# Moving the queries to the compressive memory from the projections into turns of the attention, in an attention pair on one core

## The chip, the core and the metric

One Trainium2 chip; the program runs on one of its cores. A core has TensorE (PE; its weight loads are shown as PEld), VectorE (DVE), ScalarE (ACT), GpSimd (POOL) and SyncE (SP, which here only issues DMAs); each takes its own instructions in order. The metric is device time in microseconds of a whole execution, median over runs.

## What is computed

Two attention layers stand side by side, each with 2048 tokens, 576 channels and 32 heads of 18. Their outputs are joined along the channels. A is attention of all queries over one shared head of keys and values. B works in four segments of 512 tokens: causal attention within the segment, and for each head a memory (M, z) gathered from the segments before, mixed by a gate.

```python
# A
scores = jnp.einsum("bhqd,bkd->bhqk", q, k) * (Dh ** -0.5)
o_A = jnp.einsum("bhqk,bkd->bhqd", softmax(scores), v)      # then @ wo
# B, phi(t) = t + 1 if t > 0 else exp(t), g = sigmoid(beta)
for s in range(4):
    a_dot = softmax(qs @ ks.T * scale + mask) @ vs
    num = jnp.einsum("bhld,bhde->bhle", phi(qs), M)
    den = jnp.einsum("bhld,bhd->bhl", phi(qs), z)[..., None] + 1e-6
    o = g * num / den + (1.0 - g) * a_dot                   # then @ wo
    M = M + jnp.einsum("bhld,bhle->bhde", phi(ks), vs)
    z = z + jnp.einsum("bhld->bhd", phi(ks))
```

## The kernel before

**Projections (to about 314 us).** Heads are held in five tiles of rows, four with 7 heads (126 rows) and one with 4 (72 rows); RT has the rows, t counts the tiles. Inputs and weights are split in two parts, so a projection of 512 tokens is 14 matmuls (`proj`, L239). A's four chunks come first, then B's four segments: keys and the last query tile, values (`values`, L467), the other query tiles, the bound on the scores (L530), and the update of the memory (L555 to L571). Queries, keys and values go to DRAM. For segments 1 to 3 the memory is asked here: `phi` makes phi(q) of a tile, `from_memory` multiplies it by the block-diagonal Mst (L407), scales by the gate (L411) and stores the numerator to `numB` (L412); when all five tiles are there, five products with zst (L521) give the denominators, stored to `denB` (L526). Each of these float32 products shows as two records.

**Attention (from about 314 us).** A has 32 blocks (chunk, group of four heads) of 16 key tiles, B 32 blocks of 3. The order of blocks is written out: A0, four blocks of B, A1, four of B, A2, two of B, A3, four of B, A4, two of B and so on. A block's work is cut in items (key tile, pair of heads) and these in turns of three, so an A block has 11 turns and a B block two. The first turns are 0 to 10 (A0), 11 to 18 (B), 19 to 29 (A1), 30 to 37 (B), 38 to 48 (A2), 49 to 52 (B), 53 to 63 (A3). In turn k the loop issues, in this order: the scores of turn k on PE (L845 for A, L854 for B) and their exponentials on ACT (L863), the middle one through a copy by DVE (L860); one step of the fill; one step of DVE's own exponentials; the products of turn k - 2 with the values (L893, four column tiles of 32); and what is due from a list of later steps. One item of every A block, (0, 1), has its exponential on DVE, as a polynomial of ten instructions (L818 to L828). POOL masks B's diagonals (L868).

**The fill** is the output projection of finished chunks. `out_proj` gives 60 steps of four matmuls (L742) into the single PSUM bank F; `run_fill(1)` takes one per turn. What is left at the end is made up in the tail, before the last chunk's output.

**The later steps.** When a chunk's heads 0 to 27 or 28 to 31 are done, `finish` sets down, counted in turns: d0 until the softmax sums are loaded, d1 until their inverses, d2 from a tile of heads (`load_heads`, into the tile "o" of two buffers) until its weights are loaded (tiles "rb" of ten buffers), d3 until POOL weighs it (L729). Two turns after the fifth tile, `out_proj` is put into the fill.

**Order.** PE, ACT and DVE take the attention's instructions in the order of the code (`manual_schedule`). SP's and POOL's order is made by a planner that takes the earliest instruction in the code's order whose inputs and memory it holds to be free by its own costs. A tile gets its memory from a pool, and the pools of the attention lie over those of the projections. "stA" and "P" are in one pool (`pp`), "stB", "vseg", "o", "rb", "woA" and "woB" in another (`pa`).

**Loads at the start.** Queries and keys of eight heads at a time make a stack; stB and stA have two buffers each, and the next stack is asked for when a new one is begun:

```python
    prefetch("B", 1)
    load_vseg(0)
    prefetch("B", 2)
    prefetch("A", 2)
```

A's first stack (st0) is loaded during the projections. B's output weights are loaded in turn 5, A's in turn 24.

## Time and profile before

| | us |
|---|---|
| median of three runs | 1448.38 (1448.08 to 1453.36) |
| the profiled execution | 1452.01 |
| its span, from the first to the last instruction | 1450.0 |
| PE busy in the span | 1424.0 (98%) |
| ACT busy | 1194.9 (82%) |
| DVE busy | 1023.9 (71%) |
| POOL busy | 245.7 (17%) |

Lines of the profile's views read as follows. A row of the timeline has the start and the duration in us, the engine (SPq is SP's queue of DMA issues), the line of the kernel, the operation, out<-in by the tiles' names, partitions and elements, a count where neighbours are merged, and in brackets how long the engine had been idle and what ended it. A row of the groups has the same names, a count, the busy time in us, the mean in ns of one, and the idle time before them. A row of the windows has the stretch, its length, and for PE, PEld, DVE, ACT and POOL the busy time and the number of instructions; then TensorE's granted clock, the DMA engines' busy share, and GB/s. A row of windows for one source line has PE and PEld alone. Matmuls are pipelined: the duration of one is longer than the step to the next, so costs are read from start to start.

### The profile page before, as it was taken

To read this page: it belongs to the slowest core of one execution; us is meant where nothing else is said; L and a number is where in the kernel's file an instruction comes from. 1 tells how busy PE (TensorE), PEld (TensorE's weight loads), DVE (VectorE), ACT (ScalarE), POOL (GpSimd) and SP (SyncE) were. 2 spreads that over 40 slices of the span, in tenths; PEclk is the share of its full clock that TensorE was granted. 3 is DMA by queue.
4 is the path that set the end of the run, shared out by engine and by line. 5 is a ranking of instruction groups with operands and counts; after the bars stand their busy time and mean duration, and the time that the engine had idled before them with its cause. 6 is when DMAs were issued, how large, how long until landed. Compare 5 with 4: busy or idle time off the path is not lost.

```text
span 1450.0 us, 40761 instructions
## 1 busy us (share of the span) xinstructions
PE 1424.0 (98%) x17540; PEld 840.9 (58%) x17540; DVE 1023.9 (71%) x1211; ACT 1194.9 (82%) x1429; POOL 245.7 (17%) x324
## 2 busy tenths in 40 slices
PE   9989999999999999999999999999999999999998
PEld 6768878855454555555555555555555555555565
DVE  6663473556776678887777788777778877887761
ACT  4542334259999999999999999999999999999960
POOL 2421000002123312311110160131013300100001
PEclk9999999999999999999999999999999999999999
DMA  9864444457465335332312452123104121110022
GB/s 278 270 215 137 130 162 159 162 165 202 147 175 159 92 97 175 116 108 87 108 57 68 128 154 80 62 100 93 57 26 143 60 74 46 57 42 17 17 87 74
DMA packets 86079, 166.33 MB, mean 115 GB/s; under 512 B 11872, under 2 KB 19673, under 8 KB 85718
## 3 DMA queue, kind: packets, MB, share of 16 engines
q1 hardware_dynamic: 79014, 152.87, 33.8%
q0 software_dynamic: 1664, 4.78, 1.3%
q10 hardware_dynamic: 5216, 6.03, 1.3%
q8 instruction: 138, 2.26, 0.7%
q14 instruction: 47, 0.39, 0.1%
HBM read 96.15 MB, written 67.49 MB: 113 GB/s over the span
## 4 chain that ended last, share of the span: by engine, by line
PE 64%; ACT 8%; DMA 3%; issue 2%; DVE 0%; POOL 0%; SPq 0%; DVEq 0%; POOLq 0%; ACTq 0%
PE O L893 30%; PE E L845 19%; PE F L742 11%; ACT P L863 8%; PE E L854 3%; PE E L742 1%; DMA sm<-oB 1%; PE O L742 1%; DMA rB<-sm 0%; DMA rA<-sm 0%; DMA stA<-qA 0%; DMA stB<-kB 0%; DMA stB<-qB 0%; DMA out<-osb 0%; DMA rb<-rB 0%
## 5 line engine op out<-in xcount | busy, mean ns | idle before, releaser
L863 ACT ACTIVATE P<-E 128x1024 f32<-128x1024 f32 (+1 forms) x800 | 788.4, 1078 | 15.0 <-PE E L845 11.8
L860 DVE COPY W<-E 128x1024 f32<-128x1024 f32 (+1 forms) x384 | 461.0, 1201 | 188.6 <-PE E L845 121.4
L893 PE MATMUL O<-P,VA 128*32 128x256 f32 x7936 | 509.7, 380 | 0.0
L863 ACT ACTIVATE P<-W 128x1024 f32<-128x1024 f32 (+1 forms) x384 | 434.6, 1132 | 1.5 <-DVE W L860 1.5
L893 PEld LDWEIGHTS O<-P,VA 128*32 128x32 f32 x7936 | 262.6, 110 | 146.6 <-issue 9.5
L845 PE MATMUL E<-stA,kstA 56*128 56x512 f32 x1920 | 330.8, 440 | 2.0 <-ACT P L863 1.3
L845 PEld LDWEIGHTS E<-stA,kstA 56*128 56x128 f32 x1920 | 154.6, 184 | 180.8 <-ACT P L863 121.0
L868 POOL TENSOR_SCALAR_AFFINE_SELECT P<-P 128x256 f32<-128x256 f32 (+1 forms) x192 | 94.2, 493 | 447.5 <-ACT P L863 414.7
L729 POOL TENSOR_TENSOR o<-o,rb 126x512 f32<-126x512 f32 (+1 forms) x40 | 60.5, 1518 | 436.8 <-PE F L742 143.5
L742 PE MATMUL F<-woB,o 126*32 126x192 f32 (+1 forms) x1920 | 127.6, 338 | 0.0
L825 DVE SCALAR_TENSOR_TENSOR q<-q,PD 128x1024 f32<-128x1024 f32 x96 | 118.5, 1234 | 0.0
L893 PE MATMUL O<-P,vseg 128*32 128x256 f32 (+2 forms) x1536 | 83.4, 348 | 1.9 <-POOL P L868 1.8
L742 PEld LDWEIGHTS F<-woB,o 126*32 126x32 f32 (+1 forms) x1920 | 38.2, 108 | 70.8 <-issue 61.4
L742 PE MATMUL F<-woA,o 126*32 126x192 f32 (+1 forms) x1240 | 77.7, 338 | 1.3 <-DVE osb L767 1.3
L111 ACT CAST qp<-pj 126x512 fp32r<-126x512 f32 (+1 forms) x54 | 31.3, 583 | 54.6 <-DVE kmB L423 33.2
L239 PE MATMUL pj<-xh,wBh 128*126 128x512 f32 x180 | 75.0, 416 | 0.0
L902 DVE COPY oe<-O 128x512 f32<-128x512 f32 x64 | 44.2, 691 | 41.7 <-PE O L893 39.3
L239 PE MATMUL pj<-xh,wBl 128*126 128x512 f32 x180 | 72.9, 405 | 0.0
L112 DVE TENSOR_TENSOR qp<-pj,qp 126x512 fp32r<-126x512 f32 (+1 forms) x54 | 36.7, 684 | 49.7 <-ACT qp L111 49.6
L854 PE MATMUL E<-stB 56*128 56x256 f32 (+3 forms) x512 | 62.5, 350 | 2.5 <-ACT P L863 2.0
L893 PEld LDWEIGHTS O<-P,vseg 128*32 128x32 f32 x1536 | 48.6, 110 | 27.9 <-issue 3.3
L239 PE MATMUL pj<-xl,wBh 128*126 128x512 f32 x144 | 60.0, 417 | 0.0
(177 smaller groups left out, 1372.7 us busy)
## 6 DMA issues: line engine op xcount, KB each, us to landing
stB<-kB SPq DMA_DIRECT2D x96, 144.0 KB
stB<-qB SPq DMA_DIRECT2D x32, 288.0 KB
stA<-qA SPq DMA_DIRECT2D x30, 288.0 KB
oA<-oe SPq DMA_DIRECT2D x32, 256.0 KB
oB<-oe SPq DMA_DIRECT2D x32, 256.0 KB
qA<-qp SPq DMA_DIRECT2D x16, 504.0 KB
kB<-qp SPq DMA_DIRECT2D x16, 504.0 KB
qB<-qp SPq DMA_DIRECT2D x16, 504.0 KB
```

What stands on the lines that cost most here:

```text
L112: nc.vector.tensor_tensor(qp[:R, 1, :n], src, qp[:R, 0, :n].bitcast(F32), op=ALU.subtract)
L239: nc.tensor.matmul(dst, w[:, c0 : c0 + M], x, start=i == 0, stop=i == len(ops) - 1)
L729: steps = [lambda: v.tensor_tensor(o, o, rb, op=ALU.mult)]
L742: nc.tensor.matmul(dst[32 * j : 32 * j + 32], parts[ab, c][: RT[t], t, r0 : r0 + 32], wo[ab][: RT[t], t, c0 : c0 + n], start=start, stop=stop,
L825: steps.append(lambda a=a: v.scalar_tensor_tensor(q, q, a, p, op0=ALU.add, op1=ALU.mult))
L845: nc.tensor.matmul(e[:, j], kstA[rows, 128 * kt : 128 * kt + 128], st[rows, h, :], start=True, stop=True)
L854: nc.tensor.matmul(e[:, j, c0 : c0 + 512 - 128 * k], st[rows, 4 + h, ks], st[rows, h, 128 * k :], start=True, stop=True)
L860: nc.vector.tensor_copy(src[:, :, :n], e[:, :, :n])
L863: nc.scalar.activation(p[:, :, :n], src[:, :, :n], AF.Exp, scale=SCALE)
L868: nc.gpsimd.affine_select(diag, diag, pattern=[[0, 2], [0, m], [1, 128]], base=0, channel_multiplier=-1, compare_op=ALU.is_ge, fill=0.0)
L893: nc.tensor.matmul(o[32 * j : 32 * j + 32, q0 : q0 + n], v, p[:, j % 2, p0 : p0 + n], start=m == hf == 0, stop=last and hf == 1,)
L902: nc.vector.tensor_copy(osb, o)
```

## The change

The projections no longer ask the memory. They store phi(q) of segments 1 to 3 (`qfB`, 15 stores in place of those to `numB`) and, after each update, M and z (`mzB`, two stores per segment). The matmuls of L407 and L521, their evictions and the stores to `numB` and `denB` leave the projections. Mst and zst are cleared once by POOL.

In the attention a generator `from_memory` asks the memory in 36 half tiles. For each segment these are the denominators of four tiles (t = -1) and the five tiles of numerators, the last with its own denominators; each in two halves of 256 tokens, four matmuls of 32 columns per half, into the bank F. DVE scales or adds 1e-6 and stores follow from SP. A half tile is taken in each turn from 5 on (`ASK`) whose items are all A's, in place of the fill, until all are done: turns 5 to 10, 19 to 29, 38 to 48, 53 to 60. phi(q) of a segment is loaded into a buffer of "o" (segment 1 at the start, 2 in turn 7, 3 in turn 27), M and z into the memory of woA; A's output weights are loaded in turn 92.

Blocks A0, A1 and A2 (`PLAIN`) do all their exponentials on ACT. For B's segment 0 d2 and d3 are 4 and 8 in place of 3 and 6. The heads of a new chunk are loaded only when the buffer of "o" is no longer needed for phi(q) (`place`).

```diff
+MZ = 126 + 32
+ASK, PLAIN = 5, 3
...
+    qfB = {s: dram(f"qfB{s}", [128, 5, C], F32) for s in range(1, NSEG)}
+    mzB = dram("mzB", [128, NSEG - 1, 5, MZ], F32)
...
+        nc.gpsimd.memset(Mst, 0.0)
+        nc.gpsimd.memset(zst, 0.0)
...
-            def from_memory(t):
-                R = RT[t]
-                pn = ps.tile([128, C], F32, name="mm", bufs=1)
-                nc.tensor.matmul(
-                    pn[:R], Mst[:R, t].rearrange("p h d -> p (h d)")[:, :R], fs[t][:R], start=True, stop=True
-                )
-                nm = p2.tile([128, C], F32, name="nm", bufs=2)
-                nc.vector.tensor_scalar(nm[:R], pn[:R], gt[:R, t : t + 1], None, op0=ALU.mult)
-                nc.sync.dma_start(numB[s][126 * t : 126 * t + R], nm[:R])
+            def for_memory(t):
+                nc.sync.dma_start(qfB[s][: RT[t], t], fs[t][: RT[t]])
...
-            if s:
-                pd = ps.tile([128, C], F32, name="nd", bufs=2)
-                for t in range(5):
-                    R = RT[t]
-                    nc.tensor.matmul(
-                        pd[32 * (t % 4) : 32 * (t % 4) + 32], zst[:R, t], fs[t][:R], start=t < 4, stop=t > 0
-                    )
-                dn = p2.tile([128, C], F32, name="ph_e", bufs=2)
-                nc.vector.tensor_scalar(dn, pd, 1e-6, None, op0=ALU.add)
-                nc.sync.dma_start(denB[s], dn)
...
+                nc.sync.dma_start(mzB[:, s, :, :126], Mst.rearrange("p t h d -> p t (h d)"))
+                nc.sync.dma_start(mzB[:, s, :, 126:], zst)
...
+    def load_qf(s):
+        qfs[s] = pa.tile([128, 5, C], F32, name="o", bufs=2)
+        nc.sync.dma_start(qfs[s][:126, :4], qfB[s][:126, :4])
+        nc.sync.dma_start(qfs[s][: RT[4], 4], qfB[s][: RT[4], 4])
+
+    def from_memory():
+
+        mz = pa.tile([128, 5, D], F32, name="woA").rearrange("p t d -> p (t d)")[:, : (NSEG - 1) * 5 * MZ]
+        nc.sync.dma_start(mz, mzB.rearrange("p s t m -> p (s t m)"))
+        mz = mz.rearrange("p (s t m) -> p s t m", t=5, m=MZ)
+        yield None
+        for s in range(1, NSEG):
+            qf = qfs[s]
+            for t in (-1, 0, 1, 2, 3, 4):
+                pf = psO.tile([128, C], F32, name="F")
+                for hf in range(2):
+                    cs = slice(256 * hf, 256 * hf + 256)
+                    if t < 0:
+                        cols = [(32 * i, i, 126, 32) for i in range(4)]
+                    else:
+                        cols = [(32 * j, t, 32 * j, min(32, RT[t] - 32 * j)) for j in range(4) if 32 * j < RT[t]]
+                        if t == 4:
+                            cols.append((96, 4, 126, 32))
+                    for r, i, m, n in cols:
+                        R = RT[i]
+                        nc.tensor.matmul(pf[r : r + n, cs], mz[:R, s - 1, i, m : m + n], qf[:R, i, cs], start=True, stop=True)
+                    if not hf:
+                        yield False
+                if t >= 0:
+                    R = RT[t]
+                    nc.vector.tensor_scalar(qf[:R, t], pf[:R], gt[:R, t : t + 1], None, op0=ALU.mult)
+                    nc.sync.dma_start(numB[s][126 * t : 126 * t + R], qf[:R, t])
...
+                yield True
...
+    def plain(c, hg):
+
+        return 8 * c + hg < PLAIN
...
-        dve = ab == "A" and (kt, pr) in BY_DVE
+        dve = ab == "A" and (kt, pr) in BY_DVE and not plain(c, hg)
...
     prefetch("B", 2)
+    load_qf(1)
+    memory = from_memory()
+    next(memory)
     prefetch("A", 2)
...
-        d0, d1, d2, d3 = (0, 2, 0, 3) if last else (2, 5, 3, 6)
+        d0, d1, d2, d3 = (0, 2, 0, 3) if last else (2, 5, 4, 8) if (ab, c) == ("B", 0) else (2, 5, 3, 6)
...
-            return (ab, c) in parts or len(parts) - filled[0] // FILL < 2
+            return (ab, c) in parts or len(parts) - filled[0] // FILL < 2 and asked[0] >= min(NSEG - 1, len(parts) + 2)
...
+        at(ASK + 2, 0, lambda: True, lambda k: load_qf(2))
...
-            run_fill(1)
+            if memory is None:
+                run_fill(1)
+            elif k >= ASK and k < len(turns) and all(its[n][0] == "A" for n, pr in turns[k]):
+                done = next(memory, None)
+                if done is None:
+                    memory = None
+                    run_fill(1)
+                elif asked[0] == 1 and 3 not in third:
+                    third.add(3)
+                    at(k + 3, 0, lambda: True, lambda k: load_qf(3))
...
-                    if it in (("A", 0, 0, 8), ("A", 0, 1, 8)):
+                    if it in (("A", 0, 0, 8), ("A", 0, 5, 8)):
```

More of the change, by code (lines that the diff above doesn't have):

```diff
@@ L442, in attention_pair_kernel @@
             if s:
-                from_memory(4)
+                for_memory(4)
             if s == 0:
@@ L514, in attention_pair_kernel @@
                     fs[t] = phi(pj[:126], 126, "qf", 5)
[L515 to L526 removed]
+                    for_memory(t)
             pu = ps.tile([128, C], F32, name="nd", bufs=2)
@@ L770, in out_proj @@
                 yield True
+    asked, qfs, third = [0], {}, set()
+    def load_qf(s):
[28 more added lines that the diff above has]
+                    nc.sync.dma_start(numB[s][126 * t : 126 * t + R], qf[:R, t])
+                if t < 0 or t == 4:
+                    r, n = (0, 128) if t < 0 else (96, 32)
+                    dn = pa.tile([128, C], F32, name="rb", bufs=10)
+                    nc.vector.tensor_scalar(dn[r : r + n], pf[r : r + n], 1e-6, None, op0=ALU.add)
+                    if t < 0:
+                        nc.sync.dma_start(denB[s], dn)
+                    else:
+                        nc.sync.dma_start(denB[s][7:11], dn[103:107])
+                if t == 4:
+                    asked[0] = s
+                yield True
     fill, filled, ending = [], [0], []
@@ L845, in scores @@
                 nc.tensor.matmul(e[:, j], kstA[rows, 128 * kt : 128 * kt + 128], st[rows, h, :], start=True, stop=True)
-            if (kt, pr) in BY_DVE:
+            if dve:
                 exponentials(p, e)
@@ L884, in products @@
         for j in range(4):
-            kt = turn_of[j // 2][m] if ab == "A" else m
+            kt = turn_of[j // 2][m] if ab == "A" and not plain(c, hg) else m
             p = state[b + (kt,), j // 2]
```

1 line of the change is left out of this document (removed).

## The prediction

> **What bounds the kernel now.** I read the busy time by stage first, because one average over the span hides two different kernels.
>
> ```profile
> 200.00:250.00 50.00, 50.00 (x290) 42.28 (x290) 27.48 (x68) 20.37 (x43) 0.35 (x1) 1.00 0.45 147
> 340.00:360.00 20.00, 19.21 (x268) 10.78 (x266) 11.79 (x12) 20.00 (x26) 8.87 (x18) 1.00 0.70 200
> ```
>
> In the projections (to about 314 us) PE is full and nothing else is near it. In attention's first turns ACT is full (20.00 of 20) and PE nearly so. Next the groups that the change takes out of the projections:
>
> ```profile
> L407 PE MATMUL mm<-qf,Mst 126*126 126x512 f32 x24 | 12.6, 606 | 0.0
> L521 PE MATMUL nd<-qf,zst 126*32 126x512 f32 x24 | 8.4, 605 | 0.0
> ```
>
> (each product is two records; the 72-row forms add 3.1 us to either group), and the timeline of PE around them in segment 1:
>
> ```profile
> 196.19 0.39 PE L239 MATMUL pj<-xh,wBh 128*126 128x512 f32 x1
> 196.42 1.02 PE L407 MATMUL mm<-qf,Mst 126*126 126x512 f32 x2
> 197.38 1.05 PE L521 MATMUL nd<-qf,zst 126*32 126x512 f32 x4
> 198.36 0.50 PE L239 MATMUL pj<-xl,wBh 128*126 128x512 f32 x1
> 198.69 0.39 PE L239 MATMUL pj<-xh,wBl 128*126 128x512 f32 x1
> ```
>
> Last, the start of attention: what SP issues, and what ACT and PE do meanwhile.
>
> ```profile
> 317.84 0.36 SPq L131 DMA_DIRECT2D stA<-qA  x1
> 318.56 0.31 SPq L131 DMA_DIRECT2D stB<-qB  x1
> 332.60 7.85 SPq L141 DMA_DIRECT2D stB<-shB  x4
> 346.39 0.28 SPq L132 DMA_DIRECT2D stA<-qA  x1
> ```
> ```profile
> 314.60:327.90 13.30, 7.09 (x30) 3.49 (x30) 0.74 0.54 131
> ```
> ```profile
> 327.94 1.08 PE L845 MATMUL E<-st,kstA 56*128 56x512 f32 x6
> 328.95 1.57 PE L893 MATMUL O<-P,VA 128*32 128x256 f32 x24
> 330.45 1.33 PE L845 MATMUL E<-st,kstA 56*128 56x512 f32 x6
> ```
> ```profile
> 329.28 1.96 ACT L863 ACTIVATE P<-E 128x1024 f32<-128x1024 f32 x2
> 332.03 1.07 ACT L863 ACTIVATE P<-E 128x1024 f32<-128x1024 f32 x1
> ```
>
> Apart from one early piece of A's stack, SP issues in the order of the code: B's first stack, the values, B's second stack, the rest of A's. It is at the rest of A's at 346.39. Six score matmuls make a turn; the window row counts 30 of them (L845) before 327.9, five turns, so 327.94 is turn 5 and 330.45 turn 6. ACT does a turn of three exponentials in 332.03 - 329.28 = 2.75 us, 0.918 each.
>
> **The change part by part.** *1. The projections lose the asking.* From 196.19 to 198.69 stand two steps of L239 that take 0.23 each when nothing is between (196.42 - 196.19), so one numerator tile and four denominator records cost 2.50 - 0.46 = 2.04. One numerator tile by itself:
>
> ```profile
> 183.09 0.40 PE L239 MATMUL pj<-xh,wBh 128*126 128x512 f32 x1
> 183.32 1.08 PE L407 MATMUL mm<-qf,Mst 126*126 126x512 f32 x2
> 183.83 0.80 PE L239 MATMUL pj<-xl,wBh 128*126 128x512 f32 x1
> 184.47 0.40 PE L239 MATMUL pj<-xh,wBl 128*126 128x512 f32 x1
> ```
>
> 1.38 - 0.46 = 0.92. So a denominator record costs (2.04 - 0.92) / 4 = 0.28. Three segments have 15 tiles and 30 records: 13.8 + 8.4 = 22.2. Since PE is full, nearly all of it should come off; I take **-21.5**. Bounds: -27 by the groups' busy time, -17 if PE meets waits that this work covers today. In exchange SP gets 15 stores of phi(q) of the size of the 15 numerator stores that go, and six stores of M and z for three of denominators; with the transfers at 0.45 of their time there I cost them at nothing, like the two memsets on an idle POOL. If SP lagged there, the q and k stores behind it would be late, and only the last segment's could then show, by a few us.
>
> *2. Attention has to wait for its new loads.* The code puts phi(q) of segment 1 (1.03 and 0.15 MB by their shapes) and M and z (1.21 MB) behind B's second stack. SP gets there where it issues the rest of A's stack today, 346.39. PE needs them right after the scores of turn 5, at 328.95: its order is fixed, so the products of turn 3 and the scores of turn 6 stand behind the waiting matmul, ACT has only turn 5 left (to about 333), and DVE and POOL wait for ACT. When do 2.4 MB land? The rates of the transfers in that stretch:
>
> ```profile
> 333.00:336.00 3.00, 2.83 (x35) 1.38 (x30) 2.10 (x3) 3.00 (x5) 0.00 (x0) 1.00 0.94 319
> 348.00:351.00 3.00, 2.99 (x48) 1.50 (x36) 1.87 (x2) 3.00 (x5) 2.07 (x5) 1.00 0.68 197
> 354.00:357.00 3.00, 2.97 (x49) 1.85 (x52) 2.00 (x3) 3.00 (x5) 1.97 (x4) 1.00 0.98 269
> ```
>
> At 240 GB/s, between the three, they take 10 us: landed at 357. At 319 it is 354, at 197, with the last of B's keys ahead of them, 361. Their rows are long (8 and 9 KB), which speaks for the faster half; the keys ahead speak for the slower. Restarted, PE is slow, as after its pause at 313:
>
> ```profile
> 320.20 2.79 PE L893 MATMUL O<-P,VA 128*32 128x256 f32 x24
> 324.18 1.50 PE L893 MATMUL O<-P,VA 128*32 128x256 f32 x24
> ```
> ```profile
> 319.00:320.00 1.00, 0.95 (x4) 0.51 (x4) 1.00 (x1) 1.00 (x2) 0.00 (x0) 0.50 0.51 162
> ```
>
> The granted clock is 0.50, and the same 24 records take 2.79 in place of 1.50. So turn 6 is scored at 357 + 0.9 (a half tile has 8 records, 2.79 / 3) + 2.8 = 360.7 where it was 330.45: **+30**. Bounds: +22 (landed by 351 and no slow clock: 351 + 0.5 + 1.5 - 330.45) and +34 (landed at 361); nothing if the loads come first (a rival).
>
> The Trainium skill would land the loads sooner (DMA: Bandwidth & Descriptors, Bandwidth, Measured): 1 MB in 6.15 us, 341 GB/s, on a quiet chip. By that estimate 2.4 MB take 7 us and the whole sum falls by 3; no window of this stretch reaches that rate.
>
> *3. 36 turns get a half tile.* It runs in turns 5 to 10 (A's block 0), 19 to 29, 38 to 48 and 53 to 60, and at 61 the fill takes over. Once attention is full, a turn reads:
>
> ```profile
> 572.85 0.95 PE L845 MATMUL E<-stA,kstA 56*128 56x512 f32 x6
> 573.74 0.53 PE L742 MATMUL F<-woB,o 126*32 126x192 f32 x8
> 574.08 1.48 PE L893 MATMUL O<-P,VA 128*32 128x256 f32 x24
> 575.50 0.97 PE L845 MATMUL E<-stA,kstA 56*128 56x512 f32 x6
> ```
>
> 0.89 + 0.34 + 1.42 = 2.65, PE back to back. A half tile has the shape of a third of the products: 1.42 / 3 = 0.47, so a turn with it takes PE 2.78. Without fill ACT sets the turn: 31 exponentials over 11 turns, 31 x 0.918 / 11 = 2.59. So up to 0.19 x 35 = 6.6 us more; at the least nothing, if PE's slack in these turns takes it. I take **+5**. This covers the third edit too: with 32 exponentials on ACT in blocks 0 to 2 a block takes 29.4, a turn 2.67, still below 2.78. Were PE the faster one, it would cost 3 x 0.918 = 2.75. The ten polynomial instructions that DVE loses per block, for one copy, ran beside ACT (DVE is busy 11.79 of 20 above), and the evictions that it gets (15 tiles and 6 denominators) fit there. The stores of these tiles join SP's queue.
>
> *4. The fill starts later.* By the turn numbers (heads of B's segment 0 weighed at 58 instead of 55, memory done at 61) it starts 3 steps later, and those are made up in the tail:
>
> ```profile
> 1408.43 1.84 PE L742 MATMUL F<-woA,o 126*32 126x192 f32 x40
> 1410.06 1.84 PE L742 MATMUL O<-woA,o 126*32 126x192 f32 x40
> ```
>
> 40 records are five steps and take 1.63, PE without a gap: 3 x 0.33 = **+1**. A's output weights load some 90 turns before they are used; no cost, and a stall of a load's length if not.
>
> *5. B's segment 0 gets slack.* Today POOL's weighing waits for the inverses and B's masks stand behind it:
>
> ```profile
> 440.80 1.29 POOL L729 TENSOR_TENSOR o<-o,rb 126x512 f32<-126x512 f32 x1 [25.77 <-DMA rb<-rB]
> 450.24 1.51 ACT L863 ACTIVATE P<-E 128x768 f32<-128x768 f32 x2 [3.04 <-PE E L854]
> ```
>
> ACT loses 3.04 us. Later weighing may clear this; but its heads now wait for a buffer that the memory's second segment holds until turn 44, which may move it into the masks again. Between -3 and +4; I take 0.
>
> **Sum:** -21.5 + 30 + 5 + 1 + 0 = +14.5 on the profiled span of 1450.0 (its execution took 1452.01; the runs' median is 1448.38). On the median: **1463 us**, 1.0% slower. The likeliest case's own range is 1453 to 1474.
>
> **The rivals.** *Loads in time* (0.13): SP sends phi(q) and M before B's stacks, or PE meets them ready. For it: B's stacks are needed only at turn 11, and one piece of A's stack does overtake. Against: that piece goes to another pool's memory; B's stacks and the new loads share one. Then no stall but the slow start's 2 us: -21.5 + 5 + 1 + 2 = -13.5, **1435**. This ends on the other side, and it decides as soon as the loads are issued before about 322 (7 to 10 us to land before 329 to 332).
>
> *Half the stall* (0.09): the loads land around 348, because SP gets through B's second stack sooner (at 332.60 it stands 7.85 us over four small loads). 22 + 5 + 1 - 21.5 = +6.5, and with the 3 us of part 5 off about **1452**: no change. For it is only that wait.
>
> *SP loses its lead* (0.08): besides the stall. SP runs ahead of the turns today:
>
> ```profile
> 368.55 2.96 SPq L675 DMA_DIRECT2D woA<-a_wo  x5
> 371.61 0.32 SPq L131 DMA_DIRECT2D stB<-qB  x1
> ```
>
> The code asks for this stack in turn 30, and 371.61 is 16 turns of 2.75 behind turn 5. If the stores of the tiles, which wait for DVE turn by turn, stand before such loads, a stack has four turns, some 10 us, for what took (346.39 - 318.56) / 2 = 14 at the start: 4 us at each of three places, 12 in all, **1475**. It decides once a lead falls under 14 us. Against it: SP takes what is ready, and the stall gives it 25 us of lead.
>
> **How the numbers follow.** The forecast has 0.70, the rivals 0.13, 0.09 and 0.08. A change under 0.5% (7.2 us) can't be told from none here: faster is below 1441, slower above 1456. Faster gets nearly all of the first rival, 0.12; no change most of the second, 0.01 of the first and the low edge of the forecast, 0.12; slower the rest, 0.76. The range has to take in the first rival to leave out no more than 2 in 10: 1434 to 1474.
>
> **What would show it.** The two L407 and L521 groups gone and attention starting near 293 in place of 314.6 (step 1). A gap of 24 to 28 us on ACT after its 18th exponential, ended by PE's F, whose matmul waited for the load of M and z; the granted clock at 0.50 behind it (step 2). Turns of 2.78 in blocks 1 and 2 (step 3). The first fill near turn 61 (step 4), and a gap on ACT near turn 52 or none (step 5). No gap at turn 5 makes the forecast wrong, and so does one under 15 us.

## The result, and the profile after

| | before | after |
|---|---|---|
| median of the runs (us) | 1451.33 (six runs, 1448.08 to 1453.36) | 1489.35 (six runs, 1487.80 to 1493.05) |
| ratio, with its 95% interval | | 1.0267 (1.0249 to 1.0286) |
| the profiled execution | 1452.01 | 1488.46 |
| its span | 1450.0 | 1486.7 |
| PE / ACT / DVE busy | 1424.0 / 1194.9 / 1023.9 | 1418.8 / 1198.2 / 1001.0 |

The change made the kernel 2.7% slower: 36.7 us of span, where the prediction had 14.5. PE is busy for 5 us less, so the time went into waits.

**Where the time went.** Everything of the attention runs in one fixed order on DVE, and every block ends with one copy of its output from PSUM (L902 before, L945 after). So the n-th such copy can be set against the n-th of the other kernel, and the difference of the two is the lag up to that block. Here are, from the timelines, the first exponential and the ends of A's block 0, of the fourth block of B behind it, of the first and the second block of B in the next group, of A's block 2, of the second block of B behind that, and of the last block. First the kernel before:

```profile
315.26 3.95 ACT L863 ACTIVATE P<-E 128x1024 f32<-128x1024 f32 x4 [1.34 <-PE E L845]
348.80 0.69 DVE L902 COPY oe<-O 128x512 f32<-128x512 f32 x1 [0.83 <-DMA stB<-kB]
367.46 0.69 DVE L902 COPY oe<-O 128x512 f32<-128x512 f32 x1 [0.43 <-PE O L893]
400.75 0.69 DVE L902 COPY oe<-O 128x512 f32<-128x512 f32 x1 [0.34 <-PE O L893]
405.22 0.69 DVE L902 COPY oe<-O 128x512 f32<-128x512 f32 x1 [0.59 <-PE O L893]
443.56 0.69 DVE L902 COPY oe<-O 128x512 f32<-128x512 f32 x1 [0.78 <-PE O L893]
456.04 0.69 DVE L902 COPY oe<-O 128x512 f32<-128x512 f32 x1
1404.01 0.69 DVE L902 COPY oe<-O 128x512 f32<-128x512 f32 x1 [3.31 <-PE O L893]
```

and the same places after:

```profile
300.50 1.94 ACT L906 ACTIVATE P<-E 128x1024 f32<-128x1024 f32 x2 [7.03 <-PE E L888]
366.63 0.69 DVE L945 COPY oe<-O 128x512 f32<-128x512 f32 x1 [0.73 <-PE O L936]
385.95 0.68 DVE L945 COPY oe<-O 128x512 f32<-128x512 f32 x1
419.62 0.69 DVE L945 COPY oe<-O 128x512 f32<-128x512 f32 x1 [0.34 <-PE O L936]
435.46 0.69 DVE L945 COPY oe<-O 128x512 f32<-128x512 f32 x1 [0.87 <-PE O L936]
474.18 0.69 DVE L945 COPY oe<-O 128x512 f32<-128x512 f32 x1 [0.78 <-DMA o<-oB]
491.42 0.68 DVE L945 COPY oe<-O 128x512 f32<-128x512 f32 x1
1439.76 0.69 DVE L945 COPY oe<-O 128x512 f32<-128x512 f32 x1 [0.94 <-PE O L936]
```

| up to | lag (us) | step | what lies in it |
|---|---|---|---|
| first exponential | -14.8 | -14.8 | projections, and the passage to the attention |
| end of A's block 0 | +17.8 | +32.6 | the wait at turn 5, and the slow start behind it |
| fourth block of B | +18.5 | +0.7 | |
| first block of B's next group | +18.9 | +0.4 | A's block 1 with half tiles |
| second block of that group | +30.2 | +11.3 | a wait in front of turn 34 |
| A's block 2 | +30.6 | +0.4 | half tiles again |
| second block behind it | +35.4 | +4.8 | a wait in front of turn 52 |
| last block | +35.7 | +0.3 | the other 51 blocks |
| end of the span | +36.7 | +1.0 | the tail |

A step is the difference of two rounded lags. All of the loss but 1.3 us is in by 491 us. Behind that the kernels run alike for 950 us, and the ledger leaves four places to read.

**The passage.** After, from the timeline, SP's last store of the segment (shB), ACT's last copy of the projections and PE's first scores (the first exponential stands above); last, the same store and copy of the kernel before:

```profile
291.89 1.48 SPq L526 DMA_DIRECT2D shB<-shp  x1
293.08 0.40 ACT L470 COPY vch<-pj 128x288 f32<-128x288 f32 x1 [1.46 <-PE pj L468]
298.25 0.76 PE L888 MATMUL E<-st,kstA 56*128 56x512 f32 x1 [5.21 <-DMA shB<-shp]
299.71 1.61 PE L888 MATMUL E<-st,kstA 56*128 56x512 f32 x5 [0.69 <-SPq L573]
```
```profile
307.98 0.38 SPq L535 DMA_DIRECT2D shB<-shp  x1
313.52 0.40 ACT L469 COPY vch<-pj 128x288 f32<-128x288 f32 x1 [1.47 <-PE pj L467]
```

The copy comes 20.4 us earlier, nearly the 21.5 of the prediction. But from it to the first exponential it is 1.74 us before and 7.42 after (300.50 - 293.08). PE is through with the projections and waits for the last store of the segment (shB) to land, then for SP, which stands at the branch (L573) in eight waits from 295.3 to 299.8, probably for its last stores to land. The store left SP 5.5 us ahead of ACT's last copy before the change (313.52 - 307.98), and PE worked on the values meanwhile; after, it leaves 1.2 us ahead.

**The wait at turn 5.** After: SP's issues from the start of the attention, PE's first half tile, and ACT's gap.

```profile
303.02 0.36 SPq L137 DMA_DIRECT2D stB<-qB  x1
315.67 8.48 SPq L147 DMA_DIRECT2D stB<-shB  x4
330.11 0.31 SPq L769 DMA_DIRECT2D o<-qfB  x1
330.88 0.36 SPq L775 DMA_DIRECT2D woA<-mzB  x1
344.90 1.08 PE L792 MATMUL F<-o,woA 126*32 126x256 f32 x8 [30.45 <-DMA woA<-mzB]
346.85 1.06 ACT L906 ACTIVATE P<-W 128x1024 f32<-128x1024 f32 x1 [30.19 <-PE O L936]
```

SP spends 27 us on B's two stacks and the values, and only then issues the loads for which PE has been waiting since 314.4. They need 14 us. A window of the stretch (columns as before: the granted clock, the DMA engines' share and GB/s stand last) says that the transfers are not what is scarce: while SP works through the second stack the DMA engines are half idle (0.55 here, 0.38 in the next 5 us), and the clock is at 0.50.

```profile
320.00:325.00 5.00, 0.00 (x0) 0.00 (x0) 0.00 (x0) 0.00 (x0) 0.00 (x0) 0.50 0.55 129
```

**The wait in front of turn 34.** Counted by its exponentials, the gap stands before the first of turn 34, where B's fourth stack comes into use (the expectations below, written before it was counted, say turn 32). After: SP, PE and ACT.

```profile
408.15 0.31 SPq L798 DMA_DIRECT2D numB<-o  x1
408.64 0.31 SPq L769 DMA_DIRECT2D o<-qfB  x1
409.43 0.38 SPq L137 DMA_DIRECT2D stB<-qB  x1
425.97 0.76 PE L897 MATMUL E<-stB 56*128 56x512 f32 x1 [6.42 <-DMA stB<-ones_d]
429.42 1.72 ACT L906 ACTIVATE P<-E 128x1024 f32<-128x1024 f32 x2 [8.63 <-PE E L897]
```

B's fourth stack, issued at 371.61 before, is issued at 409.43, behind the load of phi(q) of segment 3 and stores of half tiles, each of which waits on SP for DVE in its turn (19.5 us of such waits between 380 and 412). PE waits 6.42 us for one piece of it and 1.8 for the next.

**The wait in front of turn 52** ("near turn 50" in the expectations). After, from POOL's timeline and ACT's:

```profile
476.73 1.27 POOL L722 TENSOR_TENSOR o<-o,rb 126x512 f32<-126x512 f32 x1 [31.76 <-DMA rb<-rB]
479.56 3.52 POOL L911 TENSOR_SCALAR_AFFINE_SELECT P<-P 128x256 f32<-128x256 f32 x8
483.71 1.56 ACT L906 ACTIVATE P<-E 128x768 f32<-128x768 f32 x2 [5.89 <-PE E L897]
```

The same picture as before the change (3.04 us there): POOL waits for the inverses with a weighing, and eight masks pile up behind it. The inverses come later now: the weighing starts 35.9 us later than before (440.80 there), where the lag at that place is 30.6. ACT's gap is 2.9 us longer; what makes up the other 1.9 us of this step was not followed.

**The turns.** After, A's block 1, from PE's timeline:

```profile
391.53 0.97 PE L888 MATMUL E<-st,kstA 56*128 56x512 f32 x6
392.43 0.64 PE L792 MATMUL F<-o,woA 72*32 72x256 f32 x8
392.88 1.49 PE L936 MATMUL O<-P,VA 128*32 128x256 f32 x24
394.30 0.98 PE L888 MATMUL E<-st,kstA 56*128 56x512 f32 x6
```

A turn with a half tile takes 394.30 - 391.53 = 2.77 us, the 2.78 of the prediction. From 389 to 400 both PE and ACT are busy for 11.00 of 11 us.

### The profile page after: what moved, and what is told of

It is laid out like the page before. It is cut to its first block, busy times and chain, and to the rows that moved or that the text cites. A ratio compares the mean times of both kernels' runs of the same rounds, so it can differ in the third digit from the quotient of the medians.

```text
span 1486.7 us, 41304 instructions
## 1 busy us (share of the span) xinstructions
PE 1418.8 (95%) x17768; PEld 843.8 (57%) x17768; DVE 1001.0 (67%) x1190; ACT 1198.2 (81%) x1432; POOL 246.4 (17%) x326
## 4 chain that ended last, share of the span: by engine, by line
PE 65%; ACT 6%; DMA 5%; issue 2%; DVE 1%; SPq 1%; POOL 0%; POOLq 0%; DVEq 0%; ACTq 0%
PE O L936 30%; PE E L888 19%; PE F L735 10%; ACT P L906 6%; PE E L897 3%; DMA stB<-qB 2%; PE F L792 1%; PE E L735 1%; DMA woA<-mzB 1%; DMA stB<-kB 1%; DMA rb<-rB 1%; PE O L735 1%; DMA rA<-sm 0%; DVE W L903 0%; SPq L659 0%
## 5 line engine op out<-in xcount | busy, mean ns | idle before, releaser
L906 ACT ACTIVATE P<-E 128x1024 f32<-128x1024 f32 (+1 forms) x800 | 784.1, 1066 | 35.7 <-PE E L888 19.5
L906 ACT ACTIVATE P<-W 128x1024 f32<-128x1024 f32 (+1 forms) x387 | 432.7, 1118 | 32.5 <-PE O L936 30.2
L735 PE MATMUL F<-woB,o 126*32 126x192 f32 x1880 | 125.1, 338 | 0.0
L868 DVE SCALAR_TENSOR_TENSOR q<-q,PD 128x1024 f32<-128x1024 f32 x87 | 110.6, 1271 | 0.0
L735 PEld LDWEIGHTS F<-woB,o 126*32 126x32 f32 x1880 | 37.2, 108 | 69.0 <-issue 60.4
L945 DVE COPY oe<-O 128x512 f32<-128x512 f32 x64 | 44.2, 691 | 39.9 <-PE O L936 38.3
L117 ACT CAST qp<-pj 126x512 fp32r<-126x512 f32 (+1 forms) x54 | 31.0, 583 | 42.9 <-DVE kmB L424 30.2
L897 PEld LDWEIGHTS E<-stB 56*128 56x128 f32 x512 | 40.0, 191 | 39.0 <-ACT P L906 18.8
```

The costliest lines, as they stand in the source:

```text
L735: nc.tensor.matmul(dst[32 * j : 32 * j + 32], parts[ab, c][: RT[t], t, r0 : r0 + 32], wo[ab][: RT[t], t, c0 : c0 + n], start=start, stop=stop,
L868: steps.append(lambda a=a: v.scalar_tensor_tensor(q, q, a, p, op0=ALU.add, op1=ALU.mult))
L897: nc.tensor.matmul(e[:, j, c0 : c0 + 512 - 128 * k], st[rows, 4 + h, ks], st[rows, h, 128 * k :], start=True, stop=True)
L906: nc.scalar.activation(p[:, :, :n], src[:, :, :n], AF.Exp, scale=SCALE)
L945: nc.vector.tensor_copy(osb, o)
```

## The experiments

Kernels with the same projections end them up to 3 us apart from one execution to the next (ACT's last copy at 293.1 in the changed kernel, at 296.3 in the latest of the others), so a single end time can't tell 4 us. The column "attention" below takes that out: the start of the last block's copy less the start of the first exponential, both from the trace of the one profiled execution. "Passage" is the first exponential less ACT's last copy of the projections.

| kernel | end (us) | attention | passage | gaps on ACT in the attention, over 2 us |
|---|---|---|---|---|
| before | 1451.33 | 1088.7 | 1.7 | 3.0 at 52 |
| the change | 1489.35 | 1139.3 | 7.4 | 30.2 at turn 5, 8.6 at 34, 5.9 at 52 |
| loads_first | 1462.32 | 1111.9 | 6.8 | 3.0 in turn 21, 8.0 at 34, 5.3 at 52 |
| early_stacks | 1497.52 | 1146.9 | 7.2 | 28.8 at 5, 9.0 in A's block 2, 6.8 at 52, two of 3.2 and 2.4 later |
| pool_stores | 1485.45 | 1134.9 | 6.9 | 30.2 at 5, 6.9 at 52, 4.0 in A's block 3 |
| no_phi3 | 1486.47 | 1137.0 | 6.2 | as the change; 4.4 at 52 |
| act_loads | 1460.34 | 1107.8 | 8.5 | 8.5 at 34, 5.8 at 52 |
| act_pool | 1463.80 | 1111.5 | 9.2 | 3.3 at 5, 7.3 at 52, 4.0 in A's block 3 |
| late_weigh | 1493.54 | 1138.9 | 8.4 | as the change |
| plain0 | 1489.58 | 1138.7 | 6.9 | as the change; 4.4 at 52 |
| act_third | 1448.80 | 1097.0 | 8.0 | 2.1 in turn 21, 5.7 at 52 |
| third_pool | 1443.91 (9 runs) | 1093.0 | 9.3 | 2.4 in turn 21 |
| seg3_proj | 1445.36 (10 runs) | 1092.2 | 1.7 | none |
| pool_loads | 1446.95 (12 runs) | 1094.4 | 6.8 | 2.9 in turn 21 |

Without a count the end is that of one execution; before and the change have six runs each. The kernel before itself took 1452.65 us beside the kernels from loads_first to no_phi3, 1447.53 beside those from act_loads to plain0 (one execution each), and as the median of 17 runs 1450.07 beside those from act_third to seg3_proj and 1449.28 beside pool_loads.

**The wait at turn 5: loads_first and act_loads.** The first puts the loads ahead of B's stacks on SP, the second leaves SP's order and gives them to ACT's queue.

```diff
+    load_qf(1)
+    memory = from_memory()
+    next(memory)
     prefetch("B", 1)
     load_vseg(0)
     prefetch("B", 2)
-    load_qf(1)
-    memory = from_memory()
-    next(memory)
     prefetch("A", 2)
```

> The changed kernel with phi(q) of segment 1 and M and z loaded ahead of B's two stacks and the values. Theory (the gap of 30 us at turn 5 is only the place of these loads in SP's order): the gap goes, the first half tile finds its data, about 1457 to 1460 us. Rival (the stretch is short of transfer time whatever the order: some 2.4 MB more have to land before turn 15): the gap moves to B's first stack at turn 11, 10 us or more of it come back there, 1468 us or more.

```diff
     def load_qf(s):
+        queue = nc.scalar if s == 1 else nc.sync
         qfs[s] = pa.tile([128, 5, C], F32, name="o", bufs=2)
-        nc.sync.dma_start(qfs[s][:126, :4], qfB[s][:126, :4])
-        nc.sync.dma_start(qfs[s][: RT[4], 4], qfB[s][: RT[4], 4])
+        queue.dma_start(qfs[s][:126, :4], qfB[s][:126, :4])
+        queue.dma_start(qfs[s][: RT[4], 4], qfB[s][: RT[4], 4])
...
-        nc.sync.dma_start(mz, mzB.rearrange("p s t m -> p (s t m)"))
+        nc.scalar.dma_start(mz, mzB.rearrange("p s t m -> p (s t m)"))
```

> The changed kernel with phi(q) of segment 1 and M and z issued by ACT's queue before its first exponential, SP's order left as it is without them. Theory (the stall at turn 5 is made of SP's queue, where the loads stand behind 26 us of small loads, and not of transfer time): they land within 12 us of the start, the gap at turn 5 falls from 30 us to under 4, and B's stacks are not late at turns 11 and 15; about 1457 us, some 3 below the version that loads them first on SP. Rival (transfer time: both queues now share the DMA engines in the first 15 us): a gap of 5 us or more stays at turn 5, or comes at turn 11; 1465 us or more.

Both take the wait away, and B's first stack is not late in either: loads_first keeps 27.4 of the attention's 50.6 us of loss off (1139.3 - 1111.9), act_loads 31.5. Their ends, 1462.32 and 1460.34, are 2 and 3 us above what the theory had. From act_loads, PE's first half tile without an idle time in front of it, a window just after its loads were issued (302.8 to 304.5), and the late stack with the wait before turn 34, which is still there:

```profile
319.62 0.64 PE L793 MATMUL F<-o,woA 126*32 126x256 f32 x8
```
```profile
308.00:311.00 3.00, 2.88 (x14) 1.18 (x18) 1.23 (x1) 3.00 (x4) 0.00 (x0) 0.50 1.02 359
```
```profile
383.33 0.39 SPq L137 DMA_DIRECT2D stB<-qB  x1
403.14 1.02 ACT L907 ACTIVATE P<-E 128x1024 f32<-128x1024 f32 x1 [8.54 <-PE E L898]
```

So the stall was the place of the loads in SP's queue: the same bytes land in time once they are asked for in time, with 359 GB/s in these 3 us and 219 on average from 302 to 317. Two things follow. The Trainium skill says that starting DMAs on several engines saves only the time to initiate them, usually small beside the DMA (DMA: Bandwidth & Descriptors, Issuing engines are not separate DMA queues). For the transfers this trace agrees; for the waits that stand in the one queue it does not: three loads moved to another queue were worth 31.5 us of attention, and 27.4 when they were only moved ahead in the same one. And the wait at turn 34 is as long without the stall as with it (8.54 and 8.63). The prediction had thought that the stall would give SP a lead; it gives none.

**The wait in front of turn 34: early_stacks, pool_stores, act_pool, act_third.** early_stacks asks for B's next stack whenever a block of A begins:

```diff
             now[0] = k
+            if k < len(turns) and its[turns[k][0][0]][::3] == ("A", 0):
+                prefetch("B", begun[0] + 2)
+            for n, pr in turns[k] if k < len(turns) else []:
+                if its[n][0] == "B":
+                    begun[0] = 1 + keys["B"].index(("B", its[n][1], its[n][2] // 2))
```

> The changed kernel, with B's next stack asked for when a block of A begins (the buffer is free from then on) and not when the next stack of B begins, so that it stands in SP's order ahead of the half tiles' stores. Theory (SP loses its lead because loads stand behind stores that wait for their turn): the gap of 8.63 us on ACT before B's turn 32 goes, and most of the shift of 11.3 us there; about 1477 us. Rival (the transfers themselves are slower in that stretch because there are more bytes): the gap stays above 5 us, 1485 us or more. The gap at turn 5 stays at 30 us under both.

pool_stores gives the four kinds of half-tile stores to POOL:

```diff
-                    nc.sync.dma_start(numB[s][126 * t : 126 * t + R], qf[:R, t])
+                    nc.gpsimd.dma_start(numB[s][126 * t : 126 * t + R], qf[:R, t])
...
-                        nc.sync.dma_start(denB[s], dn)
+                        nc.gpsimd.dma_start(denB[s], dn)
                     else:
-                        nc.sync.dma_start(denB[s][7:11], dn[103:107])
+                        nc.gpsimd.dma_start(denB[s][7:11], dn[103:107])
```

> The changed kernel with the half tiles' stores (numB, denB) issued by POOL and not by SP. Theory (stores that wait in SP's queue cost SP its lead): the fourth stack of B is asked for before 395 and not at 409, the gap of 8.63 us goes or falls below 3, about 1478 us. Rival (it is phi(q) of segment 3, loaded in the code before the stack, that waits for its buffer): the gap stays, since that load still stands ahead of the stack on SP; 1486 us or more.

act_pool has both that and ACT's loads, and phi(q) of segments 2 and 3 on POOL too.

> As the version with ACT's loads, and besides the half tiles' stores and phi(q) of segments 2 and 3 issued by POOL, so that SP has only what it had before the change. Theory (SP's lead is lost to what the change put into its queue): neither the gap at turn 5 nor the one before turn 32 is there; what stays is the gap of some 5 us near turn 50; about 1445 us, below the kernel before. Rival (POOL's issues wait in its order and hold up B's masks, or disturb DVE, as where a DVE step of 1.2 us took 4.9 beside them): new gaps of 8 us or more, 1453 us or more.

act_third has ACT's loads and asks early for one stack only:

```diff
             now[0] = k
+            if k < len(turns) and its[turns[k][0][0]] == ("A", 0, 1, 0):
+                prefetch("B", 4)
```

> The version with ACT's loads, and B's fourth stack alone asked for at the start of A's block 1 (turn 19), so that it stands in SP's order ahead of the half tiles' stores. Theory (the gap of 8.5 us before turn 32 is SP's order alone; the version that asked for all stacks early lost it again because the softmax sums then stood behind later stacks): the gap goes and no other comes, 8 us less, about 1452 us. Rival (the wait moves again, to the sums of B's segment 0 or to the fifth stack): a new gap of 4 us or more between turns 32 and 60, 1456 us or more.

In all four the gap at turn 34 is gone: the order of SP made it. Three of them bought something else for it. In early_stacks the end rose to 1497.5, because the next early stack now stands ahead of the loads of the softmax sums on SP. DVE takes its instructions in the order of the code, so its reciprocal waits for them, and the copies for ACT stand behind it:

```profile
459.20 0.95 DVE L692 RECIPROCAL sm<-sm 112x128 f32<-112x128 f32 x1 [8.84 <-DMA sm<-oB]
461.83 1.06 ACT L906 ACTIVATE P<-W 128x1024 f32<-128x1024 f32 x1 [8.95 <-DVE W L903]
```

pool_stores has 4.4 us less attention, where its theory had 11 (1478); the fourth stack went out at 402.52, in time but not before 395. It stands there right behind the load of phi(q) of segment 3, issued at 401.71, so the load that the rival named stands in the way too, but not for long enough to make a gap. pool_stores and act_pool have a new gap of 4.0 us on ACT in A's block 3. There one step of DVE's polynomial (L870 in the first, L871 in the second), 0.68 us at the median of its 29 and not the 1.2 of the expectation, takes 4.89 beside POOL's weighing and stores. From act_pool:

```profile
478.40 4.89 DVE L871 TENSOR_SCALAR n<-n 128x1024 int32<-128x1024 f32 x1
478.49 1.29 POOL L722 TENSOR_TENSOR o<-o,rb 126x512 f32<-126x512 f32 x1
479.71 0.53 POOL L807 DMA_DIRECT2D denB<-rb  x1
480.25 2.49 POOL L722 TENSOR_TENSOR o<-o,rb 126x512 f32<-126x512 f32 x2
```

act_pool ended at 1463.80, where its theory had 1445. POOL's issues did disturb, as its rival had it, though in gaps of 3 to 7 us and not of 8: 3.3 at turn 5, 7.3 at turn 52, where POOL's masks stand behind the weighing and a store, and the 4.0. act_third has the gap gone and no new one above 2.1: 10.8 us less attention than act_loads, and 1448.80 in its one execution, level with the kernel before (1450.07, from 1446.02 to 1454.77).

**The wait in front of turn 52: late_weigh and third_pool.** late_weigh makes d3 of B's segment 0 14 in place of 8.

> The changed kernel with B's segment 0 weighed 14 turns after its inverses are asked for, not 8. Theory (the gap of 5.89 us near turn 50 is POOL's weighing, which waits for the inverses with B's masks behind it): weighing falls behind the masks, the gap goes, the fill starts 6 turns later and gives back some 2 us at the end; about 1485.5 us. Rival (the masks are late for another reason, as the late stack of B): the gap stays at 5 us or more, 1490 us or more.

The theory was right about POOL and wrong about the handle. In late_weigh the weighing stands where it stood, and the gap is 5.7:

```profile
478.73 1.27 POOL L722 TENSOR_TENSOR o<-o,rb 126x512 f32<-126x512 f32 x1 [31.52 <-DMA rb<-rB]
```

The numbers are those of the rival, but not for its reason, as third_pool shows. d3 moves the weighing in the code, but POOL's order is the planner's, which puts it where it believes the inverses to be there. The step only delays the fill (first step at 549.5, 513.5 in the change), and the tail takes 4 us more. third_pool is act_third with POOL in the code's order:

```diff
-    with tc.manual_schedule(engines={ENG.PE, ENG.Activation, ENG.DVE}):
+    with tc.manual_schedule(engines={ENG.PE, ENG.Activation, ENG.DVE, ENG.Pool}):
```

> The version with ACT's loads and the early fourth stack, and POOL in the order of the code, so that the weighing stands behind B's masks. Theory (the gap near turn 50 is the planner's place for the weighing: two multiplications that wait for late inverses stand before the masks): the gap of 5.8 us goes, about 1446 to 1448 us, level with the kernel before. Rival (the weighing falls elsewhere between masks, or the fill comes later): it is not gained, or lost again at the end, 1451 us or more.

The gap is gone: the weighing now starts behind the last mask of the group, and its wait for the inverses (6.24 us before the second row) holds up nothing.

```profile
447.63 2.98 POOL L722 TENSOR_TENSOR o<-o,rb 126x512 f32<-126x512 f32 x2
456.85 5.34 POOL L722 TENSOR_TENSOR o<-o,rb 126x512 f32<-126x512 f32 x3 [6.24 <-DMA rb<-rB]
```

third_pool takes 1443.91 us against 1450.07 for the kernel before on the same chip, a ratio of 0.9956 (0.9938 to 0.9974): 0.4% below it, a small difference, but one that the interval sets apart from none. Not all of it need belong to the moved queries. The kernel before has a wait of its own at this place (3.04 us), which POOL in the code's order would perhaps take away too: from the end of A's block 2 to the end of the second block of B behind it, it takes 12.5 us, third_pool 10.0. The kernel before with that order was not run, so how much of the 6.2 us the change is worth stays open.

**The passage: no_phi3, seg3_proj, pool_loads.** no_phi3 leaves out the stores of phi(q) of segment 3 and loads segment 2's in their place:

```diff
             def for_memory(t):
-                nc.sync.dma_start(qfB[s][: RT[t], t], fs[t][: RT[t]])
+                if s < 3:
+                    nc.sync.dma_start(qfB[s][: RT[t], t], fs[t][: RT[t]])
```

> The changed kernel without the five stores of phi(q) of segment 3 in the projections; the attention loads segment 2's in their place, so B's memory term of segment 3 is made from the wrong queries. Theory (the 7.03 us that ACT waits between projections and attention are the last stores, which the shorter projections no longer cover): 1.2 MB less at some 250 GB/s, so the first exponential comes 4 to 5 us earlier, near 296, and the end 4 to 5 us earlier, 1484 us. Rival (a fixed cost of the branch that reads the flag): the first exponential stays near 300.5, 1489 us.

It fits neither: the first exponential comes at 302.05, and the passage is 6.2 us, 1.2 less than in the change, not 4 to 5 and not 0. In the five kernels with the change's own code there (loads_first, early_stacks, pool_stores, late_weigh, plain0) it is 6.8 to 8.4, so the bytes are a small part of it. What the passage goes with is how far ahead of ACT's last copy the store of shB leaves SP: 5.5 us before the change, 1.2 after, 2.4 in no_phi3. From that store to PE's second score matmul it is 5.9 to 8.8 us in all fourteen kernels. No run moves this store alone. seg3_proj turns the question round. It is third_pool with the asking for segment 3 back in the projections, as before the change, so the work on PE returns:

```diff
+                if s < NSEG - 1:
+                    nc.sync.dma_start(qfB[s][:R, t], fs[t][:R])
+                    return
+                pn = ps.tile([128, C], F32, name="mm", bufs=1)
+                nc.tensor.matmul(
+                    pn[:R], Mst[:R, t].rearrange("p h d -> p (h d)")[:, :R], fs[t][:R], start=True, stop=True
+                )
...
-        for s in range(1, NSEG):
+        for s in range(1, NSEG - 1):
             qf = qfs[s]
...
-            return (ab, c) in parts or len(parts) - filled[0] // FILL < 2 and asked[0] >= min(NSEG - 1, len(parts) + 2)
+            return (ab, c) in parts or len(parts) - filled[0] // FILL < 2 and asked[0] >= min(NSEG - 2, len(parts) + 2)
```

> As that version with POOL in the code's order, and the memory asked for segment 3 in the projections as before the change; only segments 1 and 2 are asked in the attention. Theory (the end of the last segment's asking costs almost nothing in the projections, since without it ACT waits 5 to 7 us there for the last stores): the asking adds 7.4 us of PE work, the wait between projections and attention falls from 6 us to under 2, so the first exponential comes only 1 to 3 us later; with 12 half tiles fewer the end is 0 to 3 us earlier than without, about 1445 us. Rival (the wait is fixed, from the branch): the first exponential comes 6 to 8 us later, 1452 us or more.

From seg3_proj, ACT's last copy and first exponential:

```profile
305.55 0.40 ACT L480 COPY vch<-pj 128x288 f32<-128x288 f32 x1 [1.47 <-PE pj L478]
307.29 1.94 ACT L928 ACTIVATE P<-E 128x1024 f32<-128x1024 f32 x2 [1.33 <-PE E L910]
```

The projections end 9.3 us later than in third_pool (296.30 there) and the attention starts 1.7 us later (305.56 there). Both figures hold up to 3 us of difference between executions, but the passages alone say the same: 7.4 us of work on PE come back, and the passage falls from 9.3 to 1.7. Some 2.5 us of that are not the stores: in third_pool ACT issues its three loads ahead of its first exponential (pool_loads, below), in seg3_proj only behind it. Against pool_loads the passage falls by 5.1. The store of shB leaves SP 4.7 us ahead of ACT's last copy here. So the passage is a latency that PE work covers or leaves bare: taking the asking of the last segment away gains some 2 us of its 7.4. The 12 half tiles fewer were worth 0.8 us of attention, and the end, 1445.36 (ratio 0.9970, 0.9952 to 0.9988), can't be told from third_pool's.

pool_loads gives ACT's three loads to POOL, since in third_pool ACT's first exponential stands behind their issue:

```profile
302.62 0.58 ACTq L770 DMA_DIRECT2D o<-qfB  x1
303.61 1.68 ACTq L776 DMA_DIRECT2D woA<-mzB  x1
305.56 1.02 ACT L907 ACTIVATE P<-E 128x1024 f32<-128x1024 f32 x1 [8.87 <-PE E L889]
```

> The version with the early fourth stack and POOL in the order of the code, with the three loads (phi(q) of segment 1, M and z) issued by POOL in place of ACT. Theory (in that version ACT issues them from 302.6 to 305.3 and its first exponential stands behind them, 3 us later than its scores are ready): the first exponential comes about 1 us after the scores, 2 to 3 us earlier, and they still land before turn 5; about 1441.5 us, 0.6% below the kernel before. Rival (POOL's own issues are slower to land): a gap of 3 us or more at turn 5, 1444 us or more.

The passage falls by 2.5 us, as expected, and no gap comes at turn 5. The attention is 1.4 us longer, and the runs don't show the gain: 1446.95, ratio 0.9984 (0.9965 to 1.0003), on another chip than third_pool's. Whether it is any better stays open.

**The turns: plain0.** PLAIN is 0, so DVE keeps its polynomial in A's blocks 0 to 2.

```diff
-ASK, PLAIN = 5, 3
+ASK, PLAIN = 5, 0
```

> The changed kernel with PLAIN at 0: DVE takes its exponential in A's blocks 0 to 2 again, as before the change. The prediction's step 3 (PE sets a turn with a half tile, 2.78 us): A's blocks 1 and 2 stay as long as they are, about the same time. Rival (ACT sets these turns, with 32 exponentials in place of 31): each of the three blocks gets 0.6 to 0.9 us shorter, 2 to 2.7 us in all, 1487 us; more than 1491 us would mean that DVE is late in these turns.

From copy to copy A's blocks 1 and 2 take 29.3 and 29.4 us in the change, 29.1 and 30.1 in plain0, 28.7 each before. They don't get shorter by the rival's 0.6 to 0.9 with an exponential less on ACT, but block 2 can't decide: ACT waits 1.5 us in it for a copy that stands behind DVE's polynomial. In the change PE (29.2 and 29.4 us busy) and ACT (29.3 and 29.2) fill these blocks alike, so that PE alone sets them, as the prediction had it, is likely and not shown.

## Why the prediction was wrong

It had the sign and the largest term, and missed the size: 1463 us against 1489.35, outside its range. Of these 26 us some 3 are the kernel before, whose median was 1448.38 on three runs and 1451.33 on six; the rest is the change. The steps, by the span:

1. **Projections, -21.5: measured -14.8.** The price of the asking was about right: ACT's last copy comes 20.4 us earlier, and 17.2 to 19.8 earlier in the ten other kernels with the same projections. The step that failed is "nearly all of it should come off": its lower bound of 17 was for waits inside the projections, and the passage behind them was not looked at. There the passage grew by 5.7 us (7.4 - 1.7), since the last segment's work no longer covered the landing of the stores; seg3_proj, with that work back, has 1.7 again. The gain is measured as the first exponential moves, not as PE's busy time falls.
2. **The wait at turn 5, +30: measured +32.6** with the restart (gap 30.2, ended by PE, whose half tile waited for M and z). The issue of the loads (330.1; 346.39 less the 14.8 is 331.6) and the clock of 0.50 behind them (346 to 349) are as written; their landing took 14 us, not 10.6. The sum's reading of transfer rates was beside the point: the stretch was short of SP's issues. An estimate by the Trainium skill's 341 GB/s (DMA: Bandwidth & Descriptors, Bandwidth, Measured) lands them in 7 us, further off still. No window that the prediction showed reached this rate, but the traces have it: 372 GB/s in the kernel before from 309 to 312, and 359 in the window of act_loads above. From 340 to 346, where the loads land in the change, it was 206.
3. **Half tiles, +5: measured 1.3 in blocks 1 and 2.** The turn of 2.77 us is right, but a block has 32 items in turns of three, 10.7 turns and not 11, and was 28.7 us before: blocks 1 and 2 cost 0.6 and 0.7, block 0's six turns lie in the step above, and the eight in block 3 show nothing.
4. **The fill, +1: measured +1.0** in the tail.
5. **B's segment 0, 0 with bounds of -3 and +4: measured +4.8.** The gap grew from 3.0 to 5.9 us. The later d's could not help, since they don't decide where POOL weighs (late_weigh).
6. **The rival "SP loses its lead", given 0.08 and 12 us: it happened, with 11.3 us** at one of its three places. This is the step that failed most: the sum puts it at nothing. The reason against it was "SP takes what is ready, and the stall gives it 25 us of lead". Neither holds. The order is fixed ahead, with stores of the half tiles in front of the fourth stack, and a store that waits for DVE in turn 28 holds SP until turn 28, stall or not. act_loads shows it: without the stall the gap is the same. The mechanism and the place were written down, and so was the lead: the stack had 10.1 us (409.43 to 419.55, where PE begins to wait). The price was not: the first piece that PE waited for took 16.5 us (to 425.97), where 14 were reckoned for the whole stack, and the shift was 11.3 at one place and not 4 at each of three. That 12 came so near to it is luck.

The ledger's -14.8, 32.6, 11.3, 4.8 and 1.0, with 1.8 in its smaller steps (the half tiles of blocks 1 and 2 among them), add up to the 36.7 measured. Of the miss of 22 against the 14.5 forecast, 11.3 is this rival, 6.7 the projections with the passage and 4.8 the weighing; what the wait took more (2.6) and the half tiles took less (3.2) nearly cancel.

## What to carry to other kernels

When work moves from one stage to another, price the stage boundary it leaves: what was covered there while the work ran, and what is bare now. When it brings DMAs into a shared in-order queue, list for each what it waits for and what stands behind it; a load that is needed early belongs on a queue without waits, and a store that follows the compute turn by turn belongs behind every load that could run ahead. An idea can be sound and lose by its queue: here three loads on another queue, one stack asked for 11 turns earlier and POOL in the code's order turned 2.7% slower into 0.4% faster, with the change itself untouched. Before such a gain is put down to the idea, ask which of the repairs the kernel before could have had too: POOL's order is one.

## What the runs showed of the hardware

A DVE step of 0.68 us took 4.89 us in act_pool: it ended at 483.29, 0.55 us behind the last of three multiplications and a DMA issue that POOL ran meanwhile (to 482.74). pool_stores has the same, 4.89 us. The Trainium skill (SBUF — State Buffer, Who interferes with whom) says that a tensor_scalar of DVE can use a pair of ports that it shares with POOL, that whoever issues first has the pair for the whole instruction, and that the other is blocked. Where POOL issues no DMA, the traces agree. In plain0 the step started 0.14 us behind a multiplication, at 684.37, took 1.70 us and ended 0.56 behind it; in third_pool, at 583.43, it started 0.05 ahead of one and took 0.68. The 4.89 us are more: DVE waited for all three multiplications. This is seen only in pool_stores and act_pool, where POOL issued a store just ahead and another between. Whether these issues make the difference is not shown; DVE's record starts 0.09 us ahead of POOL's first multiplication, and whether the step had begun can't be seen.

SP's issue of four small loads (L147, 0.26 us each at the median) took 8.48 of SP's 27 us at the start of the changed kernel's attention. The trace puts 6.2 us of it down to one wait, for the load of the values (vseg) to land; why SP waits for it there was not tried.
